# The third tile's x in the list of pieces waits for the second tile's last matmul by w_in

## The chip, the cores and the metric

The kernel runs on one core of a Trainium2 chip. The metric is the device time of one execution, in microseconds (us); lower is better. Three executions of the kernel before took 867.40, 867.49 and 868.03 us, median 867.49.

## The reference

Attention within chunks of 64 positions, then a feed-forward layer with the activation h cos h:

```python
scores = scale * np.matmul(q_c, k_c.transpose(0, 1, 2, 4, 3))   # 8 batches, 8 heads, 9 chunks of 64 x 64
scores = scores - np.max(scores, axis=-1, keepdims=True)
attn = np.exp(scores)
attn = attn / (np.sum(attn, axis=-1, keepdims=True) + 1e-09)
out = np.matmul(attn, v_c)
...
h = x @ w_in            # x: 4608 tokens x 512; w_in: 512 x 2048
g = h * np.cos(h)
return (g @ w_out)      # w_out: 2048 x 512
```

## The kernel before

The 4608 tokens are worked on in 9 tiles of 512 (`TOK`). For a tile, the attention of 4 pairs of heads (`hp`) gives its x, which is kept transposed and split in two parts, a rounded `x_hi` (ScalarE, L460) and the remainder `x_lo` (VectorE, L463). Then come 16 stages, one for each block `fc` of 128 columns of w_in:

- `hidden`: 12 matmuls (four blocks of x by three products of parts) fill one of the two PSUM banks `h`.
- `activated`: six steps, in turn on ScalarE and VectorE: L497 (ScalarE, number of turns, reads h), L498 (VectorE, h less the turns), L499 (ScalarE, the sine), L500 (VectorE, h times it; after it the bank `h` is free), L501 (ScalarE, `g_hi`), L502 (VectorE, `g_lo`).
- `project`: 12 matmuls add the stage's g by w_out to four PSUM banks `acc`; it runs three stages later (`LAG`).

So TensorE's usual row is hidden, project, hidden, project, and a bank `h` is needed again two stages on.

The first 32 stages (numbered s) are: the first tile's blocks 0 to 7 (s = 0 to 7), all 16 blocks of the second tile (s = 8 to 23), the first tile's blocks 8 to 15 (s = 24 to 31). From s = 32 on the third tile and the others follow, in an order written out in the program. What surrounds the first 32 stages (the attention of the first three tiles, the joining and splitting of the weights that arrive by DMA: ScalarE L260, L262, L270, VectorE L255, L275, the loads) is put in order by a planner. `piece(engine, length, run, *after, ...)` adds a piece to the list `work`, with the pieces after which it can run; `in_order` draws 1500 changed sets of due times from a fixed seed, lays the pieces out by each with assumed lengths, keeps the best, and the pieces are then issued in the order of their planned starts. Each engine runs its instructions in that order. The planner knows only the dependencies it is given; the real ones (who wrote what, whose room is taken) become semaphore waits whether it knows them or not.

`attend_third` adds the pieces of the third tile's attention: scores, exponentials, quotients, transposes on VectorE (`turned`, L422), then for each group g of two head pairs the matmuls `weighted` into the banks a0 and a1, two casts L460 (x_hi) and two subtractions L463 (x_lo). Its parameter `begin` holds back its scores until a given matmul piece, and it is called when the list has come to s = 15.

The x tiles of the third tile take the room of the second tile's:

```python
        return xp.tile([P, 2, TOK], dtype, name=f"x{(t + (t > 1)) % 2}")   # x_room
```

t = 1 and t = 2 (the second and third tile) both give the name x1, and there are four such buffers, all in use by the second tile (two groups, hi and lo). So the cast L460 of the third tile's x can't write before the second tile's last `hidden`, stage 23, has read the buffer. In the list the pieces of these casts name only `weighted` as what they come after.

Of the kernel before, what the change touches and what calls it, by code (L numbers as in the profile page):

```python
# [31 lines left out]
GROUP = 8  # L32
# [12 lines left out]
PE, ACT, DVE, POOL, SP = range(5)  # L45
# [113 lines left out]
def attention_then_cos_ffn(ctx: ExitStack, tc, qT, kT, v, w_in, w_out, out, wide):  # L159
# [6 lines left out]
    NFC, NCC = w_in.shape[1], w_in.shape[2]  # L166
# [140 lines left out]
    def bank(kind, i):  # L307
        if kind == "a":
            b = ps_a.tile([P, 512], F32, name=f"a{i % 2}")
        else:  # L310
            b = ps_o.tile([P, 512], F32, name=f"acc{i}")
        return b
# [28 lines left out]
    def scores(t, g, banks):  # L341

        for j in range(2):
            qt, kt = queries.pop((t, 2 * g + j))
            for c in range(NCH):
                pr, par = divmod(c, 2)
                cs, ps = slice(c * CH, (c + 1) * CH), slice(par * CH, (par + 1) * CH)
                o = (j * NPR + pr) * CH  # L350
                for h in range(2):
                    hs = slice(h * CH, (h + 1) * CH)
                    matmul(
                        banks[h][ps, o : o + CH], qt[hs, cs], kt[hs, cs], start=True, stop=True
                    )
        e = weights_of(t, g).rearrange("p a (r h) k -> p a r h k", h=2)
        found = []
        for h in range(2):
            sv = banks[h].rearrange("p (a r k) -> p a r k", a=2, k=CH)
            m = att.tile([P, 2, NPR], F32, name="m", bufs=4)  # L360

            def largest(m=m, sv=sv):
                kept(nc.vector.tensor_reduce(out=m, in_=sv, op=ALU.max, axis=AX.X))

            def below(m=m, sv=sv, h=h):
                mb = m.unsqueeze(3).broadcast_to([P, 2, NPR, CH])
                kept(nc.vector.tensor_tensor(e[:, :, :, h], sv, mb, op=ALU.subtract))

            found.extend((largest, below))
        return found  # L370

    def exponentials(t, *hps):

        for e in [weights_of(t, hp // 2)[:, hp % 2] for hp in hps] or [weights_of(t, g) for g in range(2)]:
            e = e.rearrange("p c k -> p (c k)" if hps else "p a c k -> p (a c k)")
            kept(nc.scalar.activation(e, e, AF.Exp, scale=SCALE))  # L376
# [8 lines left out]
    def total(t, hp):  # L385
        kept(nc.vector.tensor_reduce(out=sums_of(t)[:, hp], in_=weights_of(t, hp // 2)[:, hp % 2], op=ALU.add, axis=AX.X))  # L386
# [218 lines left out]
    def piece(eng, length, run, *after, at=0.0, lag=0.15, port=False, table=None):  # L605
        port = port or eng == POOL
        work.append([eng, length, run, [a for a in after if a is not None], at, length + lag, port, table])
        return len(work) - 1
# [28 lines left out]
    def made_by(key, run, *args):  # L637

        def go():
            made[key] = run(*args)  # L640
        return go

    def rest_of(key, i):
        return lambda: made[key][i]()
# [5 lines left out]
    for fc in range(NFC):  # L650
        s = fc if fc < GROUP else GROUP + fc
# [4 lines left out]
    for i, (name, fc) in enumerate(turn_of):  # L656
        key = ("w", name, fc)
# [72 lines left out]
    ahead = early(1)  # L730


    def attend_third(begin):
        t = 2
        below = []
        for g in range(2):
            key = ("s", t, g)
            s = piece(
                PE, 1.2, made_by(key, lambda g=g: scores(t, g, (bank("a", 0), bank("a", 1)))),
                banks_free["a", 0], banks_free["a", 1], begin, lag=0.35,  # L740
            )
            for h in range(2):
                m = piece(DVE, 0.6, rest_of(key, 2 * h), s)
                below.append(piece(DVE, 0.6, rest_of(key, 2 * h + 1), m))
                banks_free["a", h] = below[-1]
        x = piece(ACT, 1.92, lambda: exponentials(t), *below, table=AF.Exp)
        z = [None]
        for hp in range(HP):
            z.append(piece(DVE, 0.6, lambda hp=hp: total(t, hp), x, z[-1]))
        z = piece(DVE, 0.5, lambda: inverse(t), z[-1])  # L750
        q = [piece(DVE, 0.6, lambda hp=hp: quotient(t, hp), z, port=True) for hp in range(HP)]
        w = None
        for g in range(2):
            pts = []
            for hp in (2 * g, 2 * g + 1):
                key = ("t", t, hp)
                def go(key=key, hp=hp):
                    made[key] = turned(t, hp)
                    made[key][0]()
                pts.append(piece(DVE, 0.44, go, q[hp], w, *partial_out))  # L760
                for i in range(1, 8):
                    pts.append(piece(DVE, 0.44, rest_of(key, i), pts[-1]))
            key = ("x", t, g)
            w = piece(
                PE, 1.2, made_by(key, lambda g=g: weighted(t, (2 * g, 2 * g + 1), (bank("a", 0), bank("a", 1)))),
                *pts, banks_free["a", 0], banks_free["a", 1], lag=0.35,
            )
            if g == 0:
                def values_next():
                    for hp in (2, 3):  # L770
                        load_v(t, hp)
                piece(SP, 0.1, values_next, w)
            for i in (0, 2):
                hi = piece(ACT, 0.45, rest_of(key, i), w)
                banks_free["a", i // 2] = piece(DVE, 0.6, rest_of(key, i + 1), hi)
                x_done.setdefault(t, []).append(banks_free["a", i // 2])

        def queries_next():
            for hp in range(HP):
                load_qk(t + 1, hp)  # L780

        def values_after():
            for hp in range(2):
                load_v(t + 1, hp)

        piece(SP, 0.1, values_after, piece(SP, 0.1, queries_next, w))
# [8 lines left out]
    for s in range(STAGE):  # L795
        t, fc = order[s]
        key = ("h", s)
        bank_at = held.get(s - 2) if s > 1 else None
        stream = piece(
            PE, 2.72, made_by(key, hidden, t, fc), stream, split["in", fc], bank_at,  # L800
            *x_done[t], *([turned_out[0, 1]] if s < 2 else ()),
        )
        hid = stream
        if s == GROUP:
            def prefetch_third():
                for hp in range(HP):
                    load_qk(2, hp)
            piece(SP, 0.1, prefetch_third, ahead[HP - 1], stream)
        if s >= LAG:
            u = s - LAG  # L810
            tu, fu = order[u]
            free = [out_of.get((u, sub)) for sub in range(NSUB)]
            if u == 0:
                free = [banks_free["acc", sub] for sub in range(NSUB)]
            key = ("p", u)
            stream = projected[u] = piece(
                PE, 2.72, made_by(key, project, u), stream, given[u], split["out", fu], *free
            )
            if order[u + 1][0] != tu:
                for sub in range(NSUB):  # L820
                    done = piece((DVE if sub % 2 else ACT), 0.6, rest_of(key, sub), stream,
                                 *(split.values() if u > GROUP else [ahead[HP - 1]]))
                    out_of[u + 1, sub] = done
                    if u < GROUP:
                        partial_out.append(done)
                if u < GROUP:
                    def values_third():
                        for hp in range(2):
                            load_v(2, hp)
                    piece(SP, 0.1, values_third, *partial_out)  # L830
                else:
                    piece(SP, 0.1, resume, *(out_of[u + 1, sub] for sub in range(NSUB)))
        key = ("g", s)
        def begin_g(s=s, key=key):
            made[key] = activated(*order[s], made["h", s])
            made[key][0]()
        a = piece(ACT, 0.53, begin_g, hid, given.get(s - 2), lag=0.2)
        for i, (eng, length) in enumerate(((DVE, 0.6), (ACT, 0.55), (DVE, 0.6), (ACT, 0.53), (DVE, 0.6)), 1):
            a = piece(eng, length, rest_of(key, i), a, *([projected.get(s - LAG)] if i == 4 else ()), port=i == 5, table=AF.Sin if i == 2 else None)
            if i == 3:  # L840
                held[s] = a
        given[s] = a
        if s == GROUP + 7:
            attend_third(hid)

    for i in in_order(work, x_done[2]):
        work[i][2]()
# [70 lines left out]
```

## Time and profile before

| | |
|---|---|
| Median of three executions | 867.49 us |
| The profiled execution's own time | 865.84 us |
| Its span | 864.1 us |
| TensorE busy | 845.4 us (98%) |
| VectorE busy | 555.0 us (64%) |
| ScalarE busy | 389.5 us (45%) |
| GpSimd busy | 7.5 us (1%) |
| Mean granted TensorE clock | 0.996 |

The span runs from the first to the last instruction; 1.74 us of the execution's time lie around it. Times inside the trace are counted from the span's start. A row of a timeline gives start, duration, engine, line, operation, output and inputs, the count, and in brackets how long the engine had stood idle just before and what ended that. A row of waits gives who waited for whom, the sum, how often, and the longest.

### The profile page before, as it was taken

Reading aid. Unit: us, or ns where it says so; the run is one execution under the profiler, and the core shown is the slowest. Engines: PE = TensorE matmul, PEld = TensorE weight load, DVE = VectorE, ACT = ScalarE, POOL = GpSimd, SP = SyncE. Lnnn points to the kernel's source line nnn. Section 1 sums busy time; section 2 is a strip of 40 time slices with the busy share of each in tenths; the row PEclk is TensorE's granted clock in tenths of the full one; section 3 lists DMA queues with packets and bytes.
Section 4 is the critical chain, followed back from the end, with each engine's and each line's share of the span. In section 5 each row is a group of like instructions: output and inputs, shape, how many; then the busy total and the mean of one; then the engine's idle time right before and its main releaser. Section 6 shows DMA issues by size and latency. Waiting matters only on the chain.

```text
span 864.1 us, 14053 instructions
## 1 busy us (share of the span) xinstructions
PE 845.4 (98%) x5792; PEld 695.1 (80%) x5792; DVE 555.0 (64%) x942; ACT 389.5 (45%) x636; POOL 7.5 (1%) x12
## 2 busy tenths in 40 slices
PE   6999999799999999999999999999999999999998
PEld 5778888688888888888888888888888888888886
DVE  6979878644686567665776468645865577644332
ACT  5999963333433335333533353334433353333332
POOL 1020000000000000000000000000000000000000
PEclk9999999999999999999999999999999999999999
DMA  9990200320103000300130010301030010001001
GB/s 344 416 376 34 75 2 26 120 99 2 50 1 122 25 13 37 123 25 2 49 110 15 25 49 15 109 25 50 1 122 25 2 50 25 1 1 49 1 1 49
DMA packets 26559, 57.52 MB, mean 67 GB/s; under 512 B 2944, under 2 KB 2944, under 8 KB 26496
## 3 DMA queue, kind: packets, MB, share of 16 engines
q1 hardware_dynamic: 26496, 56.63, 18.1%
q8 instruction: 45, 0.74, 0.4%
q14 instruction: 18, 0.15, 0.0%
HBM read 46.14 MB, written 10.49 MB: 66 GB/s over the span
## 4 chain that ended last, share of the span: by engine, by line
PE 92%; DVE 1%; issue 0%; ACT 0%
PE acc L193 45%; PE h L193 43%; PE a L193 4%; DVE pts L422 1%; DVE x L463 0%; DVE g L498 0%; PE a L405 0%; DVE x L561 0%; ACT x L460 0%; DVE g L500 0%
## 5 line engine op out<-in xcount | busy, mean ns | idle before, releaser
L193 PE MATMUL h<-x,w_in 128*128 128x512 f32 x1728 | 417.2, 390 | 4.8 <-DVE g L500 4.8
L193 PEld LDWEIGHTS h<-x,w_in 128*128 128x128 f32 x1728 | 324.9, 188 | 72.8 <-DVE g L500 5.3
L193 PE MATMUL acc<-w_out,g_hi 128*128 128x512 f32 x1152 | 358.4, 392 | 0.0
L193 PEld LDWEIGHTS acc<-w_out,g_hi 128*128 128x128 f32 x1152 | 214.0, 188 | 45.5 <-ACT pts L559 0.3
L193 PE MATMUL acc<-w_out,g_lo 128*128 128x512 f32 x576 | 224.4, 390 | 0.0
L498 DVE SCALAR_TENSOR_TENSOR g<-g,h 128x512 f32<-128x512 int32 x144 | 98.6, 685 | 143.4 <-ACT g L497 142.5
L497 ACT ACTIVATE g<-h 128x512 int32<-128x512 f32 x144 | 85.8, 596 | 195.2 <-PE h L193 194.8
L502 DVE TENSOR_TENSOR g_lo<-g,g_hi 128x512 fp32r<-128x512 f32 x144 | 99.6, 691 | 75.3 <-ACT g_hi L501 73.1
L499 ACT ACTIVATE g<-g 128x512 f32<-128x512 f32 x144 | 91.2, 633 | 124.5 <-DVE g L498 124.4
L501 ACT CAST g_hi<-g 128x512 fp32r<-128x512 f32 x144 | 89.4, 621 | 124.6 <-DVE g L500 78.2
L500 DVE TENSOR_TENSOR g<-h,g 128x512 f32<-128x512 f32 x144 | 99.5, 691 | 53.7 <-ACT g L499 50.6
L193 PEld LDWEIGHTS acc<-w_out,g_lo 128*128 128x128 f32 x576 | 108.1, 188 | 22.8
L422 DVE STREAM_TRANSPOSE pts<-e 32x256 f32<-32x256 f32 x224 | 97.4, 435 | 3.7
L463 DVE TENSOR_TENSOR x<-a,x 128x512 fp32r<-128x512 f32 (+1 forms) x36 | 22.3, 654 | 7.7 <-ACT x L460 7.7
L386 DVE TENSOR_REDUCE z<-e 128x8 f32<-128x512 f32 x36 | 23.7, 678 | 3.2 <-ACT e L376 3.2
L255 DVE SCALAR_TENSOR_TENSOR w<-w,half 128x512 uint32<-128x512 uint32 x32 | 22.6, 713 | 2.8 <-ACT half L262 1.6
L193 PEld LDWEIGHTS a<-kt,qt 64*64 64x64 f32 x1024 | 18.3, 135 | 7.4 <-issue 5.6
L376 ACT ACTIVATE e<-e 128x1024 f32<-128x1024 f32 (+1 forms) x22 | 19.1, 900 | 9.2 <-DVE e L337 9.1
L193 PE MATMUL a<-kt,qt 64*64 64x64 f32 x1024 | 20.6, 221 | 1.6 <-DVE x L463 1.6
L193 PEld LDWEIGHTS a<-pts,vt 64*64 64x64 f32 x1056 | 17.3, 137 | 6.0 <-issue 4.6
L460 ACT CAST x<-a 128x512 fp32r<-128x512 f32 (+1 forms) x36 | 18.5, 565 | 7.7 <-PE h L193 7.2
L396 DVE TENSOR_TENSOR e<-e,z 128x512 f32<-128x512 f32 x30 | 20.3, 683 | 0.0
(50 smaller groups left out, 252.2 us busy)
## 6 DMA issues: line engine op xcount, KB each, us to landing
qt<-in_qT_dram SPq DMA_DIRECT2D x36, 256.0 KB, 4.9
kt<-in_kT_dram SPq DMA_DIRECT2D x36, 256.0 KB, 5.1
vt<-in_v_dram SPq DMA_DIRECT2D x34, 256.0 KB, 3.7
w_in<-in_w_in_dram SPq DMA_DIRECT2D x16, 512.0 KB, 9.7
w_out<-in_w_out_dram SPq DMA_DIRECT2D x16, 512.0 KB, 9.9
out_dram<-w SPq DMA_DIRECT2D x16, 256.0 KB, 2.2
out_dram<-half SPq DMA_DIRECT2D x16, 256.0 KB, 2.1
out_dram<-x SPq DMA_DIRECT2D x4, 256.0 KB, 2.0
```

The costliest lines, as they stand in the source:

```text
L193: kept(nc.tensor.matmul(*args, **kw))
L255: kept(nc.vector.scalar_tensor_tensor(bits, bits, 3, low, op0=ALU.logical_shift_left, op1=ALU.bitwise_or))
L386: kept(nc.vector.tensor_reduce(out=sums_of(t)[:, hp], in_=weights_of(t, hp // 2)[:, hp % 2], op=ALU.add, axis=AX.X))
L396: kept(eng.tensor_tensor(e, e, zb, op=ALU.mult))
L422: kept(nc.vector.transpose(out=dst[o : o + BL, :, qb], in_=src[i : i + BL, :, kb]))
L463: kept(nc.vector.tensor_tensor(lo, xq, hi.bitcast(F32), op=ALU.subtract))
L497: lambda: kept(nc.scalar.activation(n, h, AF.Identity, bias=0.25, scale=0.5 / math.pi)),
L498: lambda: kept(nc.vector.scalar_tensor_tensor(g, n, -2.0 * math.pi, h, op0=turns, op1=over)),
L499: lambda: kept(nc.scalar.activation(g, g, AF.Sin, bias=0.5 * math.pi)),
L500: lambda: kept(nc.vector.tensor_tensor(g, h, g, op=ALU.mult)),
L501: lambda: kept(nc.scalar.copy(out=g_hi, in_=g)),
L502: lambda: kept(nc.vector.tensor_tensor(g_lo, g, g_hi.bitcast(F32), op=ALU.subtract)),
```

## The change

`attend_third` gets a second parameter, a piece `room`, and the pieces of the casts of x_hi come after it too. Its call moves from the place in the list where s = 15 was just added to the place where s = 23 was, since `room` is the `hidden` piece of stage 23; `begin` is still that of stage 15.

```diff
-    def attend_third(begin):
+    def attend_third(begin, room):
+
         t = 2
...
             for i in (0, 2):
-                hi = piece(ACT, 0.45, rest_of(key, i), w)
+                hi = piece(ACT, 0.45, rest_of(key, i), w, room)
                 banks_free["a", i // 2] = piece(DVE, 0.6, rest_of(key, i + 1), hi)
...
         given[s] = a
         if s == GROUP + 7:
-            attend_third(hid)
+            begin = hid
+        if s == GROUP + NFC - 1:
+            attend_third(begin, hid)
```

No instruction is added or taken away: every engine has as many as before. But the list has another order and one more edge, so the planner's draws fall on other pieces, and nearly the whole order of the first 32 stages differs. Three places matter for the prediction. In the rows, names have the numbers of their buffers; `h_1757` and `h_1718` are stage 22's bank before and now, `h_1804` and `h_1799` stage 23's.

ScalarE at the third tile's first group of x, before:

```order
L497 ACTIVATE g_1710<-h_1679 128x512
L499 ACTIVATE g_1710<-g_1710 128x512
L501 CAST g_hi_1711<-g_1710 128x512
L460 CAST x1_1753<-a0_1719 128x8x64
L460 CAST x1_1753<-a1_1720 128x8x64
L497 ACTIVATE g_1795<-h_1757 128x512
L497 ACTIVATE g_1834<-h_1804 128x512
L499 ACTIVATE g_1795<-g_1795 128x512
```

and now:

```order
L497 ACTIVATE g_1770<-h_1718 128x512
L499 ACTIVATE g_1770<-g_1770 128x512
L501 CAST g_hi_1771<-g_1770 128x512
L497 ACTIVATE g_1830<-h_1799 128x512
L460 CAST x1_1768<-a1_1735 128x8x64
L460 CAST x1_1768<-a0_1734 128x8x64
L499 ACTIVATE g_1830<-g_1830 128x512
```

The two casts moved from ahead of stage 22's first step to behind stage 23's first step; stage 22's steps on ScalarE are now all ahead of them.

VectorE in the second tile's attention, where GpSimd makes the last two quotients after the RECIPROCAL; L463 writes the second tile's x here. Before:

```order
L391 RECIPROCAL z_720<-z_720 128x16
L275 TENSOR_TENSOR w_out3_786<-w_701,w_out3_786 128x512
L255 SCALAR_TENSOR_TENSOR w_783<-w_783,half1_90 128x512
L500 TENSOR_TENSOR g_760<-h_706,g_760 128x512
L463 TENSOR_TENSOR x1_823<-a1_789,x1_822 128x8x64
L463 TENSOR_TENSOR x1_823<-a0_788,x1_822 128x8x64
```

and now:

```order
L391 RECIPROCAL z_693<-z_693 128x16
L500 TENSOR_TENSOR g_778<-h_702,g_778 128x512
L463 TENSOR_TENSOR x1_820<-a0_785,x1_819 128x8x64
L463 TENSOR_TENSOR x1_820<-a1_786,x1_819 128x8x64
L275 TENSOR_TENSOR w_in7_848<-w_739,w_in7_848 128x512
L255 SCALAR_TENSOR_TENSOR w_853<-w_853,half0_89 128x512
```

The two steps on weights, L275 and L255, moved from behind the RECIPROCAL to behind the two L463.

VectorE at stages 9 and 10 (`h_874` and `h_872` are stage 9's bank before and now, `h_966` and `h_964` stage 10's). Before:

```order
L498 SCALAR_TENSOR_TENSOR g_979<-g_979,h_874 128x512
L275 TENSOR_TENSOR w_out7_984<-w_959,w_out7_984 128x512
L275 TENSOR_TENSOR w_out6_987<-w_962,w_out6_987 128x512
L500 TENSOR_TENSOR g_979<-h_874,g_979 128x512
L502 TENSOR_TENSOR g_lo_890<-g_888,g_hi_889 128x512
L502 TENSOR_TENSOR g_lo_981<-g_979,g_hi_980 128x512
L498 SCALAR_TENSOR_TENSOR g_1026<-g_1026,h_966 128x512
```

and now:

```order
L498 SCALAR_TENSOR_TENSOR g_984<-g_984,h_872 128x512
L275 TENSOR_TENSOR w_out7_989<-w_979,w_out7_989 128x512
L498 SCALAR_TENSOR_TENSOR g_1020<-g_1020,h_964 128x512
L500 TENSOR_TENSOR g_984<-h_872,g_984 128x512
L500 TENSOR_TENSOR g_1020<-h_964,g_1020 128x512
```

Stage 10's L498, which needs stage 10's matmuls, moved ahead of stage 9's L500, which frees the bank that stage 11 fills.

## Prediction

> **What bounds the kernel now.** I read the page's first lines, then TensorE's waits, then the timeline around the one long wait, then the windows of the start.
>
> ```profile
> span 864.1 us, 14053 instructions
> PE 845.4 (98%) x5792; PEld 695.1 (80%) x5792; DVE 555.0 (64%) x942; ACT 389.5 (45%) x636; POOL 7.5 (1%) x12
> ...
> PE h L193 <- DVE g L500: 4.8, 1, 4.8
> PE acc L193 <- DMA kt<-in_kT_dram: 4.6, 2, 4.3
> PE h L405 <- POOL e L396: 2.4, 2, 2.1
> PE a L193 <- DVE x L463: 1.8, 2, 1.6
> PE acc L193 <- ACT pts L411: 0.7, 1, 0.7
> PE a L405 <- DVE x L463: 0.7, 1, 0.7
> ```
>
> TensorE is the bound: it is idle for 18.7 us in all, and 15.0 of these are the six rows of waits. The change adds and removes no instruction, so it can only move this idle time and the clock that comes with it. The largest row is a single wait of 4.8 us of a `hidden` for an L500, that is, for a free bank h. The others belong to the start. The timeline around the long wait, from the traces of TensorE, ScalarE (ACT) and VectorE (DVE):
>
> ```profile
> 148.71 3.02 PE L193 MATMUL h<-x,w_in 128*128 128x512 f32 x12
> 151.57 0.62 PE L193 MATMUL acc<-w_out,g_hi 128*128 128x512 f32 x2
> 154.30 2.88 PE L193 MATMUL h<-x,w_in 128*128 128x512 f32 x12
> 155.63 1.08 ACT L460 CAST x<-a 128x512 fp32r<-128x512 f32 x2 [7.15 <-PE h L193]
> 156.59 1.23 ACT L497 ACTIVATE g<-h 128x512 int32<-128x512 f32 x2
> 156.74 0.69 DVE L463 TENSOR_TENSOR x<-a,x 128x512 fp32r<-128x512 f32 x1 [6.42 <-ACT x L460]
> 157.02 0.61 PE L193 MATMUL acc<-w_out,g_hi 128*128 128x512 f32 x2
> 158.59 3.13 DVE L422 STREAM_TRANSPOSE pts<-e 32x256 f32<-32x256 f32 x7
> 161.75 0.69 DVE L498 SCALAR_TENSOR_TENSOR g<-g,h 128x512 f32<-128x512 int32 x1
> 162.47 0.63 ACT L499 ACTIVATE g<-g 128x512 f32<-128x512 f32 x1 [4.66 <-DVE g L498]
> 164.00 0.68 DVE L500 TENSOR_TENSOR g<-h,g 128x512 f32<-128x512 f32 x1
> 164.74 4.44 PE L193 MATMUL h<-x,w_in 128*128 128x512 f32 x12 [4.84 <-DVE g L500]
> 169.11 1.16 PE L193 MATMUL a<-pts,vt 64*64 64x64 f32 x64
> ```
>
> Stage 22's `hidden` runs from 148.71, stage 23's from 154.30. The cast L460 stood on ScalarE ahead of stage 22's L497. It waited 7.15 us, until 155.63, which is when stage 23's first six matmuls, those that read the first group of x, are through (154.30 plus half of 2.72 is 155.66). Behind it stood L497 of stage 22, ready at about 151.7 and run at 156.59; VectorE's L498 then came behind seven transposes, at 161.75; L500 ended at 164.68; stage 24's `hidden`, which needs that bank, began at 164.74.
>
> **The change part by part.** *The casts' wait.* The regular length of a set of twelve matmuls is this row of the chain, and the clock is in the windows:
>
> ```profile
> 71.41 2.72 PE acc L193 x12
> ...
> 25.00:42.00 17.00, 17.00 (x129) 13.76 (x129) 15.88 (x26) 16.39 (x29) 0.00 (x0) 1.00 1.03 417
> 42.00:62.00 20.00, 19.34 (x152) 15.63 (x151) 15.87 (x28) 19.53 (x32) 4.77 (x4) 1.00 0.99 391
> 62.00:130.00 68.00, 68.00 (x475) 55.66 (x474) 58.75 (x97) 59.87 (x106) 0.00 (x0) 1.00 0.14 47
> 150.00:176.00 26.00, 21.16 (x145) 16.91 (x144) 14.61 (x27) 7.45 (x13) 0.00 (x0) 0.93 0.35 118
> ```
>
> (The columns behind the length are TensorE's busy time, the weight loads', VectorE's, ScalarE's, GpSimd's; then the granted clock.) Stage 24's `hidden` was due at 157.02 + 2.72 = 159.74 and began at 164.74: 5.00 us. It then took 169.11 - 164.74 = 4.37 us to the next matmul, where stage 22's took 151.57 - 148.71 = 2.86 (151.57 is where the next project began): 1.51 us more, at a granted clock of 0.93 over this window against 1.00 elsewhere. So the wait costs 6.5 us.
>
> In the new order all six steps of stage 22 are ahead of the casts. Its L500 can be done some 3 us after 151.7 (L497 0.60, L498 0.69, L499 0.63, L500 0.68, and hand-offs), 5 us before the bank is needed at 159.74. The casts stand behind stage 23's L497, which needs all twelve matmuls of stage 23, so what they wait for is over when their turn comes. Behind them stand L499 and L500 of stage 23, put off by two casts (1.08) and two L463 (0.69 and about 0.6): 2.4 us. Without it L500 would end at about 159.9; with it at 162.3; its bank is wanted by stage 25 at 159.74 + 2 x 2.72 = 165.2. Covered by 2.9 us; without cover it would cost up to 2.4. The third tile's x itself is wanted only at stage 32, 8 x 5.4 us on. I take the full 6.5.
>
> *The start, redrawn.* Here no row tells what the new order does; bounds come from the nearest rows.
>
> ```profile
> 21.02 0.74 DVE L463 TENSOR_TENSOR x<-acc,x 128x256 fp32r<-128x256 f32 x2
> 22.45 0.75 DVE L463 TENSOR_TENSOR x<-a,x 128x256 fp32r<-128x256 f32 x2
> 22.92 2.08 PE L193 MATMUL a<-kt,qt 64*64 64x64 f32 x64 [1.59 <-DVE x L463]
> 49.29 2.05 POOL L396 TENSOR_TENSOR e<-e,z 128x512 f32<-128x512 f32 x2 [34.76 <-ACT g L499]
> 56.81 2.72 POOL L396 TENSOR_TENSOR e<-e,z 128x512 f32<-128x512 f32 x2 [5.48 <-DVE z L391]
> 57.10 1.53 DVE L255 SCALAR_TENSOR_TENSOR w<-w,half 128x512 uint32<-128x512 uint32 x1
> 60.69 1.22 PE L405 MATMUL a<-ident,e 128*128 128x128 f32 x8 [0.66 <-DVE x L463]
> 72.30 0.68 DVE L500 TENSOR_TENSOR g<-h,g 128x512 f32<-128x512 f32 x1
> 73.97 1.30 PE L193 MATMUL h<-x,w_in 128*128 128x512 f32 x5
> ```
>
> (a) The second tile's first scores waited 1.59 us for the last head pair's x, which sat in the banks a. Now the third pair's sits there and the last pair's in acc, so they can start up to 1.4 us earlier (22.45 against 21.02). But ScalarE was busy for 16.39 + 19.53 = 35.9 of the 37 us that follow, with the same work now (as many table loads too), so a lead of TensorE is lost again before 62. Between -1.4 and 0 I take 0.
>
> (b) At 57.10 L255 took 1.53 us, 0.84 more than the 0.69 of its like, beside GpSimd's two quotients, which took 2.72 instead of the 2.05 of the first two. TensorE's 0.66 at 60.69 hangs on an L463 behind it. Now L500 and both L463 come first. By the row alone whatever stands there may be hit again; I take 0 between -0.84 and 0. [...]
>
> (c) Stage 9's L500 freed its bank at 72.98, and stage 11's `hidden` began at 73.97 with 1.0 us to spare. Now stage 10's L498 stands ahead of that L500, so stage 11 depends on stage 10's whole chain: from the end of its matmuls L497, L498 and L500 (0.60 + 0.6 + 0.69 and three hand-offs, about 2.0 us) against the 2.72 of the project between, with the 0.16 by which a matmul ends after its slot taken off: 0.5 to spare if neither engine is late. ScalarE is 88% busy here (59.87 of 68), and one weight step stands in between on either engine, 0.5 to 0.6 each. So 0 to 0.7 for these; I take +0.5, near the upper end, since both engines are nearly full.
>
> Sum: -6.5 + 0.5 = -6.0 us. Against the profiled execution's 865.84 (span 864.1 and 1.74 around it) that is 859.8, a span of 858.1. The median of the runs, 867.49, is 1.65 above the profiled one; for it I forecast **861.5**.
>
> **The rivals.**
>
> *TensorE waits for transposes instead.* The second `weighted` of the third tile needs the last transposes L422, and two of these now stand on VectorE behind stage 24's L498. That one comes at about 159.74 + 2.86 + 0.6 = 163.2, and two transposes (3.13 / 7 = 0.45 each) end at about 164.7; TensorE comes to `weighted` after one project, at 165.2. Cover 0.5 us. If VectorE is a few steps late, TensorE idles by up to 1.3 us (three transposes); such a short idle costs no clock (after the 1.59 above the first `hidden` had 1.00). For it: VectorE's own order has no room there. Against: it was busy for 14.6 of the 26 us from 150 to 176. Time: 862.8.
>
> *The redrawn start gives it back.* The gain is one wait, and the order of 130 us is new. If the list lets ScalarE idle for 6 us more before 62, where it had 1.1 idle, its work can be made up only in the 8 us that it had free from 62 to 130, and TensorE waits meanwhile. Time: about 867.5, no change. Against: the counts of its work and the weights' turn are the same, and only 0.66 of TensorE's idle lay between 25 and 130 before.
>
> *Slower: a weight not yet there.* The sixth w_in is read on ScalarE seven instructions earlier than before:
>
> ```profile
> w_in<-in_w_in_dram SPq DMA_DIRECT2D x16, 512.0 KB, 9.7
> ...
> 22.04 0.33 SPq L190 DMA_DIRECT2D w_in<-in_w_in_dram  x1
> 34.15 0.60 ACT L270 CAST w_out<-w 128x512 fp32r<-128x512 f32 x1
> 37.67 0.67 ACT L262 ACTIVATE half<-w_in 128x512 uint32<-128x512 uint32 x1
> ```
>
> It was read at 37.67; now right behind what ran at 34.15. Issued at 22.04 and 9.7 us under way, it lands at 31.7: 2.5 us (with an earlier start 1) in hand. In ScalarE's queue every step of g stands behind it, so TensorE would wait as long as it does. To turn the gain into a loss of 0.2% it must land 2.5 + 6.0 + 1.7 = 10.2 us late, twice its usual time: 869.2. Against: this load's queue and order are unchanged.
>
> **How the numbers follow.** The forecast has 0.82, the transposes 0.11, the start that gives it back 0.04, the late weight 0.03. The range's low end is the wait with (a) in full, -7.9, and 0.3 for the spread of runs (they lie 0.6 apart): 859.3. Its high end is the wait with (c) at 0.7, the transposes at 1.3 and 1.1 more in the start: -3.4, 864.1. Within 0.2% (1.7 us, about what a measurement of this kernel can tell from no change) lies only the start that gives it back. Faster 0.93, same 0.04, slower 0.03.
>
> **What the profile after would show.** TensorE's wait of `hidden` for L500 at 160 is gone or under 1 us, and ScalarE's 7.15 us before L460 with it; the clock in that window is 1.00. If TensorE's waits between 25 and 130 add up to more than 2 us, the start was mis-sized; if a wait of `a` for L422 appears near 165, it is the transposes. The forecast is wrong if the first 130 us get longer by more than 4 us.

## The result and the profile after

The kernel after takes 858.78 us (median of four executions, 858.60 to 859.08) against 867.61 for the kernel before beside it (867.40 to 868.03): a ratio of 0.9898, 95% interval 0.9881 to 0.9915. That is 8.8 us less. The forecast was 861.5, its low end 859.3: the direction was right, the forecast time 2.7 us too long. The profiled execution took 858.76 us, span 857.0, so it lies at the median, which that of the kernel before (865.84) did not. Two executions of about 3000 us, one of the kernel before and one of the version below with wait and start filled (its profiled one), are left out of what follows.

The page of the kernel after, with TensorE's waits:

```profile
span 857.0 us, 14052 instructions
PE 841.9 (98%) x5792; PEld 692.2 (81%) x5792; DVE 553.4 (65%) x942; ACT 390.4 (46%) x636; POOL 6.8 (1%) x12
...
PE acc L193 <- DMA kt<-in_kT_dram: 4.9, 1, 4.9
PE h L405 <- POOL e L396: 3.2, 2, 2.8
PE a L405 <- DVE x L463: 1.1, 2, 0.9
PE h L405 <- DVE e L396: 1.1, 2, 0.7
PE a L193 <- DVE x L463: 0.6, 1, 0.6
PE h L193 <- DVE g L500: 0.4, 2, 0.3
```

The 4.8 us of `hidden` for an L500 are gone; 0.4 us in two pieces is left, both in the first 75 us. The other rows are the start, in another mixture. TensorE is also 3.5 us less busy for the same 5792 matmuls (841.9 against 845.4): the windows below show the higher clock at the wait, 1.00 instead of 0.93. (A second profile of the kernel after has 1.55 us more than the first between 10 and 850 us: 834.96 against 833.41.)

The timeline of the kernel after at the third tile's first group of x:

```profile
149.99 0.60 ACT L497 ACTIVATE g<-h 128x512 int32<-128x512 f32 x1 [1.76 <-PE h L193]
152.01 0.69 DVE L500 TENSOR_TENSOR g<-h,g 128x512 f32<-128x512 f32 x1
153.77 2.88 PE L193 MATMUL h<-x,w_in 128*128 128x512 f32 x12
156.75 0.60 ACT L497 ACTIVATE g<-h 128x512 int32<-128x512 f32 x1 [2.39 <-PE h L193]
157.25 1.07 ACT L460 CAST x<-a 128x512 fp32r<-128x512 f32 x2
158.35 1.29 DVE L463 TENSOR_TENSOR x<-a,x 128x512 fp32r<-128x512 f32 x2 [0.28 <-ACT x L460]
159.21 2.88 PE L193 MATMUL h<-x,w_in 128*128 128x512 f32 x12
159.56 0.68 DVE L500 TENSOR_TENSOR g<-h,g 128x512 f32<-128x512 f32 x1
163.54 0.89 DVE L422 STREAM_TRANSPOSE pts<-e 32x256 f32<-32x256 f32 x2
164.75 1.16 PE L193 MATMUL a<-pts,vt 64*64 64x64 f32 x64
165.84 3.02 PE L193 MATMUL h<-x,w_in 128*128 128x512 f32 x12
```

Stage 22's L500 ends at 152.70; stage 24's `hidden`, which needs that bank, comes at 159.21, 6.5 us later, and waits for nothing. The casts run at 157.25 with no idle ahead of them. Stage 23's L500, put off by them, ends at 160.24 and is wanted at 165.84. The last transposes end at 164.43, and `weighted` comes at 164.75: 0.3 us of cover.

Its windows, cut as those of before, and then the first of them for the kernel before:

```profile
0.00:25.00 25.00, 15.09 (x345) 13.42 (x346) 16.59 (x33) 13.06 (x26) 2.75 (x8) 1.00 0.94 345
25.00:42.00 17.00, 16.73 (x126) 13.21 (x125) 16.49 (x28) 16.95 (x31) 0.00 (x0) 1.00 1.03 417
42.00:62.00 20.00, 18.86 (x150) 15.23 (x149) 14.47 (x26) 19.91 (x32) 4.10 (x4) 1.00 1.03 414
62.00:130.00 68.00, 67.84 (x474) 55.41 (x473) 57.91 (x96) 60.36 (x106) 0.00 (x0) 1.00 0.12 43
150.00:176.00 26.00, 26.00 (x233) 21.46 (x230) 18.14 (x33) 10.18 (x18) 0.00 (x0) 1.00 0.37 122
```

```profile
0.00:25.00 25.00, 15.39 (x337) 13.75 (x337) 16.45 (x33) 13.49 (x27) 2.74 (x8) 0.93 0.95 353
```

From 150 to 176 the granted clock is now 1.00 instead of 0.93, and so it is in the first 25 us. There the rows tell less than it seems: the record of the clock starts at 9.11 us in the profile after and at 10.80 in that of before, and what comes earlier is shown as 1.00 unmeasured. The first 32 matmuls of the first tile's scores take 1.97 us in the kernel before (0.062 each), and the 110 recorded ones in the kernel after 5.32 from 4.89 on (0.048 each), where 32 of the same size take 1.15 (0.036 each) at 26.05 in the kernel after, at a clock of 1.00. My estimate from this is that neither start is at full clock throughout; no trace has the clock there.

Where the time went, between the two profiled executions: the second tile's first scores start at 21.01 instead of 22.92 (1.91 us ahead), stage 11's `hidden` at 73.51 instead of 73.97 (0.46), stage 23's at 153.77 instead of 154.30 (0.53), and the end comes 7.1 us sooner. So 0.5 us come from the start and 6.6 from the wait. The timed runs differ by 8.8; where the other 1.7 us are was the question for the experiments.

### The profile page after: what moved, and what is told of

The parts are those of the page before. It is cut to its first block, busy times and chain, and to the rows that moved or that the text cites. A ratio compares the mean times of both kernels' runs of the same rounds, so it can differ in the third digit from the quotient of the medians.

```text
span 857.0 us, 14052 instructions
## 1 busy us (share of the span) xinstructions
PE 841.9 (98%) x5792; PEld 692.2 (81%) x5792; DVE 553.4 (65%) x942; ACT 390.4 (46%) x636; POOL 6.8 (1%) x12
## 4 chain that ended last, share of the span: by engine, by line
PE 91%; ACT 4%; DMA 2%; DVE 1%; issue 0%; SPq 0%; ACTq 0%
PE acc L193 45%; PE h L193 43%; PE a L193 4%; DMA qt<-in_qT_dram 2%; ACT half L262 1%; DMA w_in<-in_w_in_dram 1%; ACT w L260 1%; ACT g L499 0%; ACT w_out L270 0%; ACT w_in L270 0%; ACT L376 0%; ACT g_hi L501 0%; SPq L190 0%; DVE g L498 0%; ACT e L376 0%
## 5 line engine op out<-in xcount | busy, mean ns | idle before, releaser
L498 DVE SCALAR_TENSOR_TENSOR g<-g,h 128x512 f32<-128x512 int32 x144 | 98.6, 685 | 141.3 <-ACT g L497 140.5
L497 ACT ACTIVATE g<-h 128x512 int32<-128x512 f32 x144 | 86.0, 597 | 194.6 <-PE h L193 194.2
L499 ACT ACTIVATE g<-g 128x512 f32<-128x512 f32 x144 | 91.0, 632 | 120.2 <-DVE g L498 120.1
L500 DVE TENSOR_TENSOR g<-h,g 128x512 f32<-128x512 f32 x144 | 99.5, 691 | 54.1 <-ACT g L499 50.9
L422 DVE STREAM_TRANSPOSE pts<-e 32x256 f32<-32x256 f32 x224 | 97.3, 435 | 3.7
L255 DVE SCALAR_TENSOR_TENSOR w<-w,half 128x512 uint32<-128x512 uint32 x32 | 21.7, 686 | 2.3 <-ACT half L262 1.2
L463 DVE TENSOR_TENSOR x<-a,x 128x512 fp32r<-128x512 f32 (+1 forms) x36 | 22.1, 654 | 0.6 <-ACT x L460 0.5
L367 DVE TENSOR_TENSOR e<-a,m 128x512 f32<-128x512 f32 x28 | 19.1, 686 | 0.5
```

Of the source, the lines that this page charges most:

```text
L255: kept(nc.vector.scalar_tensor_tensor(bits, bits, 3, low, op0=ALU.logical_shift_left, op1=ALU.bitwise_or))
L422: kept(nc.vector.transpose(out=dst[o : o + BL, :, qb], in_=src[i : i + BL, :, kb]))
L463: kept(nc.vector.tensor_tensor(lo, xq, hi.bitcast(F32), op=ALU.subtract))
L497: lambda: kept(nc.scalar.activation(n, h, AF.Identity, bias=0.25, scale=0.5 / math.pi)),
L498: lambda: kept(nc.vector.scalar_tensor_tensor(g, n, -2.0 * math.pi, h, op0=turns, op1=over)),
L499: lambda: kept(nc.scalar.activation(g, g, AF.Sin, bias=0.5 * math.pi)),
```

## The experiments

In the diffs, `run` is the list in its final order, `put(moved, behind)` takes pieces out of it and sets them right behind another, `steps[s]` are the six steps of stage s, `casts[g]`, `rests[g]` and `turns[g]` the third tile's L460, L463 and L422 of group g. Only the lines that do the moving are shown; those that collect these lists are left out. The median of the kernel before was 867.3 us beside the first three, 867.4 beside the four from "No wait" to "The kernel after once more", 867.65 beside the other draw and the fillers with 36 calls, and 867.46 beside the last three. Behind each time stand the lowest and highest run, and the ratio to the kernel before with its 95% interval.

**The two casts alone, in the order of before.**

```diff
+    put([i for i in run if i in casts[0]], steps[23][0])
+    put([i for i in run if i in rests[0]], steps[23][1])
```

> The order of before in everything, but the third tile's first two casts L460 stand behind stage 23's L497, and their two subtractions L463 behind stage 23's L498. So the start is that of before and only the long wait goes. The wait cost 5.0 us of lateness and 1.5 us of low clock in the profiled execution; the seven transposes still stand ahead of stage 22's L498, so up to 0.9 us of TensorE's wait may stay. Theory 1 (the timed runs of before lose 1.7 us more than the profiled one in that wait, by the clock): 867.6 - 8.2 + 0.9 = 860.3 us. Theory 2 (the 1.7 us and the gain beyond 6.5 us lie in the redrawn start): 867.6 - 6.5 + 0.9 = 862.0 us.

Measured: 862.48 us (861.07 to 863.38), ratio 0.9945 (0.9931 to 0.9958). Four pieces moved past a few others bring 4.8 of the 8.8 us, nearest to the 862.0 of the second expectation. That one laid the rest of the gain in the redrawn start; the version "No wait, and the start of before" below, which keeps that start and has no wait at all, says otherwise (859.60). From the timeline:

```profile
161.70 3.02 PE L193 MATMUL h<-x,w_in 128*128 128x512 f32 x12 [0.86 <-DVE g L500]
...
165.21 1.15 PE L193 MATMUL a<-pts,vt 64*64 64x64 f32 x60 [0.24 <-DVE pts L422]
```

Two waits stay, 1.1 us together, since stage 22's L499 still stands behind stage 23's L497 and the casts, and seven transposes ahead of its L498. So the queue behind the casts mattered beside the casts themselves.

**The new order with the casts back in their old place**, ahead of stage 22's L497.

```diff
+    put([i for i in run if i in casts[0]], steps[22][0])
+    put([steps[22][0]], run[run.index(casts[0][0] if run.index(casts[0][0]) > run.index(casts[0][1]) else casts[0][1])])
+    put([i for i in run if i in rests[0]], steps[22][0])
```

> The order of the changed kernel in everything, but the third tile's first two casts L460 and their subtractions L463 are put back ahead of stage 22's L497 and L498. The cast's wait for stage 23 is back, with fewer transposes between it and stage 22's L498 than before had. Both theories: ScalarE idles some 7 us again. If that wait alone makes TensorE late, all of 5 us and the low clock come back: 865 to 867 us. If it needs the seven transposes behind it, stage 24 is late by under 1 us and only the second group's matmuls (which need the transposes that come late) wait, 2 to 3 us in all and no low clock: about 862 us.

Measured: 866.31 us (865.39 to 866.98), 0.9989 (0.998 to 0.9998): nearly all of the gain is lost again, as much as the first expectation had it but by another way. Two rows of its timeline:

```profile
167.08 0.33 PE L193 MATMUL a<-pts,vt 64*64 64x64 f32 x4 [1.51 <-issue]
170.39 1.98 PE L193 MATMUL a<-pts,vt 64*64 64x64 f32 x60 [2.98 <-DVE pts L422]
```

Stage 24's `hidden` waits only 0.2 us. The second `weighted` comes late instead, 4.5 us in two pieces: 2.98 us for the transposes, which the late steps of g have pushed back, and 1.51 ahead of its first four matmuls, for which the profile names no releaser ("issue"). Behind the first of these waits the granted clock is 0.50 from 167.8 to 174.6, 6.8 us, and 1.00 again from there.

**Seven transposes out of the way, in the order of before**; the casts stay where they were.

```diff
+    gone = run.index(steps[22][1])
+    behind = [i for i in run[:gone] if i in turns[1]][-7:]
+    put(behind, steps[22][3])
```

> The order of before, but the seven transposes L422 that stood ahead of stage 22's L498 on VectorE stand behind its L500. The casts wait as before. Stage 22's steps come 3.1 us sooner, so the one idle stretch of 4.8 us falls into two, of about 1.1 us before stage 24 and 2.4 us before the second group's matmuls. If low clock comes only with one long idle stretch, none is left here. Theory 1 (the clock after the long wait cost the timed runs 3.2 us): 867.6 - 1.3 - 3.2 = 863.1 us. Theory 2 (it cost 1.5 us as profiled): 867.6 - 1.3 - 1.5 = 864.8 us.

Measured: 867.85 us (866.52 to 868.59), 1.0006 (0.9998 to 1.0015). Both expectations failed. In its timeline the wait of `hidden` shrinks from 4.8 to 1.6 us, and the transposes that were moved are then late themselves:

```profile
162.31 3.02 PE L193 MATMUL h<-x,w_in 128*128 128x512 f32 x12 [1.57 <-DVE g L500]
...
168.99 1.97 PE L193 MATMUL a<-pts,vt 64*64 64x64 f32 x60 [3.40 <-DVE pts L422]
```

The idle is 5.0 us in all, as before; it is only cut in two. VectorE's queue was a part of the length of the wait, but moving these transposes took nothing away: ScalarE's wait stayed, 7.15 us at L460 as before.

**The kernel before once more**, for a second profile of the same program.

> The kernel before, unchanged, for a second profile of it. If the phase of the clock's low stretches differs from one execution to the next, the granted clock and the span differ from 0.996 and 864.1 us: Theory 1 expects about 865.8 us with one more low stretch near 165 us, Theory 2 the same 1.7 us more within the first 25 us.

Measured: 866.99 us, span 865.2. The wait is the same 4.8 us, and TensorE loses the same 6.6 us around it. What differs is the start, 1.15 us longer up to the first `hidden` (26.08 instead of 24.93). Windows of this execution, TensorE alone (busy time, granted clock, DMA):

```profile
18.77:22.18 3.41, 2.09 (x67) 1.00 1.04 407
22.18:25.60 3.42, 2.77 (x52) 0.50 1.02 391
```

A second stretch of half clock lies over the second tile's first scores (3.32 us instead of 2.08); in the first execution none lay there (1.00 from 22 to 26). **A third profile** told the same from the other side.

> The kernel before once more, for a third profile of it. If the low clock behind the wait is laid out anew in each execution, its length there differs from the 3.4 us of the first two, and the time between the sets of matmuls around it with it (6.6 us there so far); if it hangs on the idle alone, both are the same again.

Measured: 865.82 us, the half clock behind the wait again 3.4 us long (0.50 from 164.4 to 167.8, 1.00 on both sides), one such stretch in the start (0.50 from 14.2 to 17.6), 864.0 of span as in the first. So in three profiles of this kernel one stretch of 3.4 us lay behind the wait of 4.8 us each time, while the start had one, two and one.

**No wait, and the start of before.** Stage 22's L498 to L500 right behind its L497, the casts as in the first experiment, the second `weighted` one project later.

```diff
+    put([steps[22][1]], steps[22][0])
+    put([steps[22][2]], steps[22][1])
+    put([steps[22][3]], steps[22][2])
+    put([i for i in run if i in casts[0]], steps[23][0])
+    put([i for i in run if i in rests[0]], steps[23][1])
+    second = [a for a in work[casts[1][0]][3]][0]
+    put([second], projected[21])
+    put([i for i in run[: run.index(second)] if second in work[i][3]], second)
```

> The order of before up to stage 21, so its start, but no wait at the third tile: stage 22's L498, L499 and L500 come right behind its L497, the two casts and two subtractions behind stage 23's L497 and L498, and the second group's matmuls one project later. What is left against the changed kernel is the start alone. Theory 1 (all of the gain is the wait): as the changed kernel, 858.8 us. Theory 2 (the redrawn start is worth something): in the profiles so far the start of before has TensorE 1.2 us later at stage 43 of the sets (0.5 to 1.7) than that of the changed kernel: 860.0 us, and up to 860.8 by the times of the kernel whose casts alone were moved.

Measured: 859.60 us (859.26 to 860.42), 0.9916 (0.9903 to 0.9929), between the two expectations. Stage 24's `hidden` starts at 160.89 without a wait, and from there to the end this kernel neither gains nor loses against the kernel after. So, in timed runs, the wait with all that hangs on it is worth 7.8 us, and the redrawn start 0.6 to 0.8.

**The same with the start's idle filled**: 6 calls of a 128x128 matmul, whose result is read by nobody, in each of the two idle places before 23 us. `filled` holds a 6 for two pieces, the last of the first tile's scores and its last `weighted`.

```diff
+        if i in filled:
+            fill(filled[i])
```

> The kernel clean_start_of_before with twelve more matmuls of 128 x 128 by the identity, whose results nobody reads: six behind the first tile's scores and six behind its last matmuls by v, in the two places where TensorE is idle before 23 us. If the low clock within the first 25 us makes the start of before late (theory of the clock), the low stretches from 14 to 26 us go and it gains 0.5 to 1.2 us on clean_start_of_before. If the start is late by what ScalarE and VectorE do in their order, nothing changes (under 0.3 us), whatever the clock shows.

Measured: 859.19 us (858.62 to 859.62), 0.4 less, between the two expectations. The four runs of the one overlap those of the other, so this alone doesn't show that the start's low clock is a part of what the new start saves; 0.2 to 0.4 us against the kernel after stay, which is no more than the spread of the runs.

**The call moved, without the edge**, against the kernel after:

```diff
-                hi = piece(ACT, 0.45, rest_of(key, i), w, room)
+                hi = piece(ACT, 0.45, rest_of(key, i), w)
```

> The call of the third tile's pieces is moved as in the change, but the casts do not wait for stage 23's piece. The list is redrawn and the casts stand ahead of stage 22's L497 again, with three transposes ahead of its L498. If the edge is what gains: TensorE waits about 1 us before stage 24 and 2 to 3 us before the second group's matmuls, with two low stretches of the clock behind them: 866 to 867 us. If moving the call was enough: 858.8 us.

Measured: 865.99 us (864.30 to 869.01), 0.9987 (0.9977 to 0.9998). Its timeline on ScalarE and TensorE:

```profile
155.32 1.08 ACT L460 CAST x<-a 128x512 fp32r<-128x512 f32 x2 [6.75 <-PE h L193]
...
161.13 3.02 PE L193 MATMUL h<-x,w_in 128*128 128x512 f32 x12 [1.54 <-DVE g L500]
...
167.86 0.68 PE L193 MATMUL a<-pts,vt 64*64 64x64 f32 x28 [2.96 <-DVE pts L422]
```

Without the edge the planner puts the casts ahead of the matmuls that they wait for again, and ScalarE stands for 6.75 us. The place of the call alone is worth 1.4 us at most.

**The kernel after once more**, beside these three.

> The changed kernel, unchanged, for more of its times and clocks beside those of before on one chip. Expected 858.8 us, granted clock 0.997 to 0.999 (no low stretch but one in the start), against 0.990 to 0.996 of before.

Measured: 858.98 us (858.88 to 859.00), 0.9907 (0.9893 to 0.9922).

**Another draw**: seed 9 in place of 1 for the planner, edge and call as in the kernel after.

> The new kernel with another seed for the planner's draws (9 instead of 1), edge and call as in the new kernel. If the edge is what takes the wait away, the wait for L500 at 160 is absent here too, and the time is within 1.5 us of 858.9; if the new kernel's order was only a lucky draw, it is at 864 or more. The start can come out earlier or later by up to 1 us; if it is earlier, this beats the new kernel.

Measured: 860.18 us (859.02 to 861.83), 0.9918 (0.9903 to 0.9933); no wait for an L500 at 160. So the gain of the edge is not the luck of the first draw. But this kernel's runs lie 2.8 us apart, with mean granted clocks of 0.998 in three (859.02 to 860.18), 0.996 in one (860.23) and 0.994 in the longest. **Its start filled** as above:

> The kernel with the other draw (860.18, runs from 859.02 to 861.83) with 6 such calls each in its two idle places of the first 23 us (2.35 us ahead of the first transposes of e, 1.73 ahead of the second tile's first scores). Theory 1 (its spread is low clock of the start): its runs come within 1 us of each other, and the time is at most that of its fastest run, 858.5 to 859.0, so level with the new kernel or better. Rival (the fillers stand in the way, or the spread is not the clock's): 860 or more.

Measured: 858.98 us (858.70 to 859.50), 0.9909 (0.9895 to 0.9922). Its runs are now 0.8 us apart, so much of the spread was the clock's. It ties with the kernel after and doesn't beat it.

**The wait filled.** In the kernel before, matmuls that nobody reads, just ahead of stage 24's `hidden`: lateness stays, the idle goes.

```diff
+        if i == hid_24:
+            fill(36)
```

> The kernel before with 36 extra matmuls of 128x128 (identity by identity, into a free bank a0, about 0.11 us each, 4 us in all; their result is read by nobody) put on TensorE just ahead of stage 24's hidden, where it stood idle for 4.8 us. The lateness of that hidden stays; the idle goes. Theory 1 (what the wait costs in timed runs, 7.8 us, is 5.0 of lateness and the rest a low clock that follows the idle, more of it than the 1.5 us in the profiled execution): about 864.6, 2.7 below before, and the runs lie closer together. Theory 2 (the low clock costs the 1.5 of the profile, the rest comes from elsewhere): about 865.9. Theory 3 (the low clock doesn't hang on this idle): 867.4, as before.

Measured: 867.80 us (866.72 to 870.32), 1.001 (1.0 to 1.002). It looks like theory 3, but the filler was mis-sized:

```profile
160.14 8.20 PE L193 MATMUL a<-ident 128*128 128x128 f32 x72
168.10 2.99 PE L193 MATMUL h<-x,w_in 128*128 128x512 f32 x12
```

A call is two matmuls here, and the 72 of them kept the `hidden` back until 168.10. Stage 23's `hidden` started at 154.69 here, 0.39 us later than in the first profile of before, so the bank would have been free at about 164.74 + 0.39 = 165.1: the filler ran over by 3.0 us. The low clock behind it is gone, though (1.00 from 160 to 176): the twelve matmuls take 2.9 us to the next instead of 4.4. **With the start filled too:**

> The same, and 6 such matmuls each in the two idle places of the first 23 us, so that no long idle of TensorE is left in the first 170 us but the first. Theory 1: what is left against the new kernel is lateness alone, 5.0 of the wait and 0 to 0.6 of the start: 863.9 to 864.5, with runs that lie within 0.6 us. Theory 2: 865.3 to 865.9. Theory 3: as before, less 0.4 at most.

Measured: 867.23 us (866.93 to 868.49), 1.0002 (0.9994 to 1.0011); the mean granted clock is 0.998 to 1.000 in all its runs. Less the 3.0 us, that is 864.2. Both were made again **with 20 calls, for the wait**

> The kernel before with 20 extra calls of a 128x128 matmul (40 matmuls of 0.114 us each by the profile of the run with 36 calls, 4.6 us; their result is read by nobody) just ahead of stage 24's hidden, where TensorE stood idle for 4.8. Theory 1 (behind the wait lies more low clock in timed runs than in the profiles): 864.9, that is the run with 36 calls less the 3.0 us by which its filler ran over, with no granted clock under 0.996 but for the start's windows. Theory 2 (the low clock is worth 1.5 us in all runs): 865.9. Theory 3 (it doesn't hang on the idle): 867.4.

and **for wait and start.**

> The same with 6 calls each in the two idle places of the first 23 us. Theory 1: 864.2 to 864.4 (867.23 less the 3.0 us run over; or 858.9 + 5.0 of lateness + the start's 0.5), runs within 1 us. Theory 2: 865.3 to 865.9. Theory 3: 867.

Measured: 866.42 us (865.48 to 866.81), 0.9989 (0.998 to 0.9998) for the wait alone, and 864.98 us (864.39 to 865.37), 0.9976 (0.9967 to 0.9985), for both, which has no usable trace. The timeline of the first:

```profile
161.54 4.63 PE L193 MATMUL a<-ident 128*128 128x128 f32 x40
166.56 3.05 PE L193 MATMUL h<-x,w_in 128*128 128x512 f32 x12 [0.38 <-DVE g L500]
169.53 1.59 PE L193 MATMUL a<-pts,vt 64*64 64x64 f32 x64
```

The filler fits. The lateness is 166.56 - 161.54 = 5.02 us, as the forecast had it, and the clock is 1.00 from 160 to 172. The filled wait came out 1.5 us above theory 1 and nearer theory 2; its profiled execution has three stretches of half clock in the start, 10.2 us. With the start filled too the gain is 2.5 us, 0.6 to 0.8 short of theory 1 and 0.3 better than theory 2's best. So filling both idles, with the lateness left, takes about 2.5 us off the timed runs of the kernel before, 1.0 with the filled wait and 1.4 more with the filled start, where the same filling was worth 0.4 in the kernel without the wait.

## Why the prediction was wrong, step by step

The 8.5 us or so from 867.46 to 858.98 come apart in four medians, from two different comparisons, so each to some 0.3 us:

| | us | |
|---|---|---|
| kernel before | 867.46 | |
| no idle left in start and wait, lateness as before | 864.98 | half clock: 2.5 |
| no wait either, start of before, filled | 859.19 | lateness of the wait: 5.8 |
| kernel after | 858.98 | order of the start: 0.2 |

The split depends on the way that is taken. With the wait taken away first (867.39 to 859.60, 7.8 us), filling the start brings only the last 0.4. So half clock and lateness together come out alike both ways, 8.2 to 8.3 us; how much each has is known to about 1 us only.

- *The casts' wait: right, in mechanism and in the profile's size.* Forecast 6.5 us, measured 6.6 between the two profiled executions. Lateness 5.00 was forecast, 5.02 measured with the idle filled. Of the other 0.8 of the table's 5.8, 0.6 shows in that trace: from stage 23's `hidden` to stage 26's it takes 23.27 us where the kernel after takes 17.66, so 5.6 us. `weighted` has 0.44 of this (1.53 us to the next matmul instead of 1.09): in the kernel before the last L422 ends at 168.10, 3.42 us behind stage 22's L500, and by the same 3.42 my estimate for its end here is 169.9, 0.4 us after `weighted` begins at 169.53. In the kernel before (24.23 us) `weighted` begins only at 169.11, behind the `hidden` at half clock, and takes 1.09 us to the next matmul; so the half clock adds 1.0 us there (24.23 - 23.27) and not the 1.5 of the forecast; the sum of 6.5 was right all the same. L460's 7.15 us wait is gone, and so is L500's; the clock is 1.00. The cover for stage 23's L500, forecast as 2.9 us, is 5.6 (160.24 to 165.84): the L500 came 1.5 us sooner than worked out, and `weighted` lies ahead of stage 25.
- *The step that failed: the offset.* "The median of the runs, 867.49, is 1.65 above the profiled one" was carried over as if it lay outside the change. It went with the change: the kernel after's runs lie within 0.5 us, and its profiled execution is 0.02 us from their median. Without the offset the forecast would have been 859.8; the 1.0 us from there to 858.78 is the start's, below. What the offset was made of is shown in part: by the estimate that follows, mostly half clock. A stretch of 3.41 us at half clock is 0.002 of this kernel's mean granted clock (3.41 x 0.5 of 864.1 us), and the 81 runs of before in the four later comparisons rank by it: 866.4 us on average at 0.996 (23 runs), 867.1 at 0.994 (28; one more at 0.993), 868.0 at 0.992 (26), 868.9 at 0.990 (3). That is about 0.8 us for each stretch, and 1.1 of the 1.65 between the profiled execution's rank, 0.996, and the median; the rest is the spread inside that rank (865.43 to 867.53). With both idles filled the runs lie 1.0 us apart and 2.5 lower. In the kernel after the mean tells nothing (858.60 us at 0.997, 858.99 at 1.000): in its first profile the little that is missing was lost in the last 1.4 us, where TensorE has no work.
- *The start: wrong sign.* Forecast +0.5, measured -0.5 in the profiles. That is the other 1.0 us down to 858.76. Rows of the kernel before, then of the kernel after:

```profile
49.28 0.69 DVE L500 TENSOR_TENSOR g<-h,g 128x512 f32<-128x512 f32 x1 [0.17 <-ACT g L499]
61.67 2.52 PE L193 MATMUL h<-x,w_in 128*128 128x512 f32 x10
```

```profile
21.01 2.08 PE L193 MATMUL a<-kt,qt 64*64 64x64 f32 x64 [0.57 <-DVE x L463]
57.77 2.05 POOL L396 TENSOR_TENSOR e<-e,z 128x512 f32<-128x512 f32 x2 [7.05 <-DVE z L391]
58.19 0.69 DVE L500 TENSOR_TENSOR g<-h,g 128x512 f32<-128x512 f32 x1 [0.58 <-ACT g L499]
60.88 1.41 PE L193 MATMUL h<-x,w_in 128*128 128x512 f32 x5
73.51 2.80 PE L193 MATMUL h<-x,w_in 128*128 128x512 f32 x11 [0.16 <-DVE g L500]
```

- (a) "A lead of TensorE is lost again before 62" was half wrong. The lead was 1.91 us at the first scores, more than the 1.4 that was given as its bound, and 0.79 was left at 61 (the `hidden` behind the matmuls L405 starts at 60.88 instead of 61.67). The reason given, that ScalarE was full, did not bind it whole: ScalarE had 1.08 us idle between 25 and 62 before and 0.14 now. The difference is about what was kept; that the one explains the other is not shown.
- (b) The two quotients take 2.05 us now instead of 2.72, and L500 beside them 0.69: no hit. The prediction had no need to leave this open: in the kernel before, an L500 at 49.28 took 0.69 us beside the first two quotients, which began at 49.29 and took 2.05. The 0.84 us did not become time, however: the same matmuls L405 now wait 0.89 and 0.25 us for L463 where they waited 0.66.
- (c) Forecast +0.5, measured 0.3 (the lead falls from 0.79 to 0.46 by stage 11), 0.16 of it a wait of stage 11's `hidden` for that L500; the rest is open. Right in mechanism, as far as the 0.16 go.
- *"Such a short idle costs no clock": wrong.* In the kernel before half clock came with waits of the start, none over 3.1 us behind the first loads: in its second profile the 1.59 us ahead of the second tile's first scores end at 22.83, and the clock is 0.50 from 22.18 to 25.60. In the kernel after, a wait of 2.82 us (until 13.55) has 1.00 behind it. Seen in one execution it had looked free.
- *The rivals.* Transposes: the cover was 0.3 us where 0.5 was forecast, and it held; where the casts are late, as in three experiments, it is just there that the time goes (waits for L422 of 2.98, 3.40 and 2.96 us). The start did not give the gain back. The sixth w_in was there in time, but the third was not: in the profiled execution after, ScalarE waits 0.93 us for its load, until 22.80, which it didn't before. In the second profile of the kernel after ScalarE is idle for 0.37 us in all between 20.34 and 23.75, too little for such a wait.

What stays open: how the 8.2 us divide between half clock and lateness; why the timed runs of before have more stretches of half clock than two of its three profiles, and how much of them the start alone brings; three profiles showed one, two and one of them in the start and always one behind the wait.

## What to carry over

Before an offset between a profile and the median is added to a forecast, see whether it comes and goes with the work that the change takes away: here 1.1 of the 1.65 us was clock lost behind idle, by the estimate above, and with the wait gone and the start redrawn the kernel's profile lies 0.02 us from its median. A dependency that the planner wasn't told still bound at run time, and held up what stood behind the waiting instruction in its queue: 7.15 us at L460, and stage 22's L497, whose matmuls were through at about 151.7, behind it at 156.59. Cutting this wait in two, or moving what it held up, only moved the idle: the three versions that did so, with ScalarE's wait kept (casts back, transposes moved, no edge), saved 1.4 us at most of the 8.8.

## What the runs showed of the clock

Where it is on record, the granted clock changes in the first profile of the kernel before at 14.22, 17.63, 164.40 and 167.82 us, that is at edges of windows of 3.41 us (the 146.77 between are 43 of them), and in the second at 15.36, 18.77, 22.18 and 25.60, so the windows' places differ from one execution to the next. Cut at these edges, TensorE's busy time and clock in the kernel before (first profile):

```profile
10.80:14.22 3.42, 1.36 (x27) 1.00 1.05 405
14.22:17.63 3.41, 3.06 (x70) 0.50 1.05 401
...
160.99:164.40 3.41, 0.00 (x0) 1.00 0.00 0
164.40:167.82 3.42, 3.08 (x7) 0.50 0.00 0
```

and in the one with the transposes moved, where the idle was cut in two:

```profile
164.91:168.32 3.41, 0.69 (x6) 1.00 0.00 0
168.32:171.74 3.42, 2.75 (x62) 0.50 0.18 35
171.74:175.15 3.41, 3.41 (x9) 0.50 0.40 123
```

The windows ahead of half clock were not all idle throughout: the one at 10.80 above has 1.36 us of work. In the windows of eleven profiles cut like this, each at full clock with under 1.55 us of TensorE's work was followed by one at half clock (12 of 12), none with over 2.1 us was, and between them it went either way: behind 2.09 us in the second profile of before above came half clock, behind 1.88 in the kernel after full. At half clock, windows with 2.75 us of work or less (3 of them) were followed by another at half clock, those with 2.77 or more by full clock; 0.02 us is less than one matmul of 64x64 took there (60 of them 1.97 us, 0.033 each), so the border is not that sharp. So two idles of 1.6 and 3.4 us cost 6.8 us of half clock where one of 4.8 cost 3.4, and the 1.59 us of idle ahead of the second tile's first scores had full clock behind it in the first profile of before, with edges at 21.04 and 24.45, and half clock in the second, with edges at 18.77, 22.18 and 25.60. Why the clock falls is not shown by these runs.
